# Entry into a state-space loop on Trainium2: three sets of steps reordered, chunk 2's tables built one period sooner

## The chip, the cores and the metric

The kernel runs on one core of a Trainium2 chip. A core has a matrix engine (TensorE, PE in the profile), a vector engine (VectorE, DVE), an activation engine (ScalarE, ACT), a general engine (GpSimd, POOL) and a sync engine that mostly issues DMA transfers (SyncE, SP). Each takes its instructions strictly in the order in which they stand in the program; between engines, semaphores order the work. The metric is the device time of one execution in microseconds (us), the median of the runs shown.

## The reference

A sequence of 2048 positions with 448 channels goes through two branches, mixed by a gate; the kernel returns the mixed output and fourteen gradients.

```python
def fwd(A_u, ..., gate_w):
    x = A_u
    g = sigmoid((x * gate_w).sum(-1, keepdims=True))
    a = S4(x)          # K[d,l] = Re sum_n C dB exp(dt A l); y = causal convolution of u with K, + u * Dskip
    b = MLP(B_x)       # h = relu(x w1 + b1)**2 ; out = h w2 + b2
    return g * a + (1 - g) * b
...
out, vjp = jax.vjp(fwd, A_u, A_A_re, ..., gate_w)
return (out, *vjp(grad_out))
```

The part at issue is the S4 branch's kernel K (448 channels x 2048 positions from 256 complex modes) and, from its gradient dK, the gradients of the modes; and beside it the two layers of the MLP, forward and backward. Positions are rounded to bfloat16, so dK is first summed over positions that round to the same value.

## The kernel before

The middle third of the kernel is a loop over 14 chunks of 32 channels. For each chunk VectorE builds tables of powers: X tables (`step_x`, L656 and L657) and Y tables (`seeds_y`, `build_y`: L723, L670, L673, L679), by doubling from seeds in a record that `load_rec` brings from HBM. ScalarE spreads the record's factors first, `fields_x` (L708, L711) and `fields_y` (L716, L719). Then `kgen` (L752) multiplies X and Y to K, and `k_out` (L759) copies it out.

The backward half of a chunk needs Y transposed (YT). For chunk 0 TensorE turns it (`turn_y`: transposes L788, ScalarE copies L789); for later chunks a DMA transpose does (`load_yt`, L778). `back_z` multiplies YT by a scaled dK (TensorE L814, ScalarE copy L816), `turn_x` turns X (L772), `back_p` multiplies the two on VectorE (L826, L827), `back_s` sums over modes (L843). Scaled dK comes from `scale_a` (ScalarE L795) and `scale_v` (VectorE L799). `psF`, one PSUM tile, is shared by `back_z` and `turn_x`.

**The entry.** Ahead of the loop stand: tables of chunk 0; tables of chunk 1; 116 small matmuls with the weights `Ew` (L1036) that sum the gradient, loaded in four quarters (`load_hs`, L312), to dK; six casts of the sums (L1043); their writes to the scratch tensor `dk_d` (L1047, L1049); two reads of `dk_d` into DK (L1052, L1053), 40 rows and one, on two copies of the partitions; a zeroed row block (L1059, L1060); chunk 0's Y turned; dK scaled; `kgen(0)`.

**The loop.** A string `PERIOD` gives the order of the steps of one period: forward tables of chunk c, backward of chunk c-1, and in between, at each `D`, some steps of the MLP (`dense`). Of the 127 dense steps seven make a block's first layer (`first_layer`: matmuls L904, L907; two ScalarE relus L911; a store L912; two steps later VectorE's square L914) and eight the second (`project`: L880, L882; copy L886; each step half of one output tile). `first_steps = 8` of them fall to period 1; the rest is spread evenly over periods 2 to 13. In period 1 the tables of chunk 1 stand already, so the names in `BUILT` are left out there. The second layer's weights (`w2n`, L1147) are loaded in period 1.

Instructions stand on each engine in the order in which the Python text issues them (`manual_schedule`).

Of the kernel before, what the change touches and what calls it, by code (L numbers as in the profile page):

```python
# [12 lines left out]
ACT = mybir.ActivationFunctionType  # L13
# [6 lines left out]
P = 128  # L20
# [308 lines left out]
def kernel(ctx, tc, A_u, A_A_re, A_A_im, A_B_re, A_B_im, A_C_re, A_C_im, A_log_dt, A_Dskip,  # L329
# [302 lines left out]
    DK = KW[:, NA * D:].rearrange("p (a d) -> p a d", d=D)  # L632
    for h in range(2):
        G_.memset(KW[64 * h + 32:64 * h + 64, NA * D:].bitcast(fp32), 0.0)
    RB = K.t("R32", [P, 16384])
# [215 lines left out]
    w1w = KW[:, 0:7168].rearrange("p (a f) -> p a f", a=DT)  # L851
# [13 lines left out]
    lates = []  # L865

# [28 lines left out]
    def first_layer():  # L895

        rx = [SB[:, 8192:9216], SB[:, 9216:10240], hv[:, 7168:8192], st4]
        for lb in range(4):
            for jp in range(HP):
# [10 lines left out]
                for k in range(2):  # L910
                    S.activation(r[:, 512 * k:512 * k + 512], pss[k][:], ACT.Relu, bias=b1_f[:, 2 * jp + k:2 * jp + k + 1])  # L911
# [84 lines left out]
    for q in range(4):  # L996
        K.load_hs(hd[0], q, hss[q])
    kps = [None]
# [8 lines left out]

    seeds_x(0)
# [5 lines left out]
    load_rec(1)  # L1014
    tables(0)
    fields_x(0)
    fields_x(1)
    tables_y(0)
    nc.sync.dma_start(w1w[:, 0:3], bass.AP(tensor=B_w1.tensor, offset=B_w1.offset, ap=[[F, P], [P * F, 3], [1, F]]))
    for h in range(2):  # L1020
        nc.sync.dma_start(w1w[64 * h:64 * h + 64, 3], bass.AP(tensor=B_w1.tensor, offset=B_w1.offset + 384 * F, ap=[[F, 64], [1, F]]))
# [3 lines left out]
    for i in range(3):  # L1025
        fields_y(i)
    tables_y(1)
# [7 lines left out]
    for k, (x8, g, e, gr) in enumerate(ekeys):  # L1035
        T_.matmul(tiles[e][32 * gr:32 * gr + 32, 0:D], lhsT=ct["Ew"][:, 32 * k:32 * k + 32], rhs=hss[x8 // 2][:, g, x8 % 2, :], start=(k == first[e, gr]), stop=(k == last[e, gr]),  # L1036
                  tile_position=(0, 32 * gr), skip_group_check=True)
    stA, stB = (K.t("st", [P, 4, D], bufs=2) for i in range(2))
    for e in range(6):
# [4 lines left out]
        for l in range(2 if e < 2 else 1):  # L1044
            q = G_ if (e + l) % 2 == 0 else nc.scalar
# [4 lines left out]
    for cpy in range(2):  # L1050
        qe = nc.scalar if cpy else G_
        qe.dma_start(DK[64 * cpy:64 * cpy + 40], bass.AP(tensor=dk_d, offset=0, ap=[[16 * D, 40], [D, 16], [1, D]]))  # L1052
        qe.dma_start(DK[64 * cpy + 40:64 * cpy + 41, 0], bass.AP(tensor=dk_d, offset=640 * D, ap=[[D, 1], [1, D]]))  # L1053

# [4 lines left out]
    G_.memset(zrow, 0.0)  # L1059
    nc.scalar.dma_start(bass.AP(tensor=k_d, offset=16 * 48 * D, ap=[[D, 48], [1, D]]), zrow)  # L1060
# [13 lines left out]
    def spare():  # L1074

        xst[0] += 1
        return K.ps("SX"[xst[0] % 2], [P, 8, P], bf16)
# [561 lines left out]
```

## Time and profile before

| | us |
|---|---|
| median of 3 runs | 816.03 (811.8 to 819.44) |
| profiled execution, its own time | 817.63 |
| its span in the profile | 815.8 |
| TensorE busy in the span | 621.9 (76%) |
| VectorE busy | 625.3 (77%) |
| ScalarE busy | 506.0 (62%) |
| GpSimd busy | 163.9 (20%) |

A row of the timeline gives start, duration, engine, line, operation, what is written and read, the count of instructions merged into it, and in brackets the idle time of the engine just before it with what ended that. `<-DMA` names a transfer that landed. Of a row that merges instructions the duration runs from the first one's start to the last one's end. A row of the windows gives a stretch and its length, then for PE, PEld (weight loads), DVE, ACT and POOL the busy time with a count, then the clock that TensorE was granted (1.00 is full), the share of the DMA engines in use, and GB/s. A row of the groups gives line, engine, operation, tiles and shapes, count, busy us in all, mean ns of one, and idle time before.

### The profile page before, as it was taken

The page shows a single profiled execution, that of the slowest core. Times are in us where ns is not written, and L with a number is a line of the kernel's source. Part 1 is how long each engine was busy: PE and PEld are TensorE (multiplying, and loading weights), DVE is VectorE, ACT ScalarE, POOL GpSimd, SP SyncE. Part 2 cuts the span into 40 slices and gives each one's busy share as a digit, 9 for nine tenths or more (in the row PEclk, how much of TensorE's full clock was granted, in tenths as well). Part 3 has the DMA queues.
Part 4 walks back from the last instruction along what each step waited for, and adds up shares of the span by engine and source line. Part 5 has one row for each costly group of instructions (what it writes and reads, how often), then busy time and mean ns, then how long its engine had stood idle before and what let it go on. Part 6 is the DMA issues. An engine that isn't in the chain of part 4 may idle for free. (4 is left out here: it accounts for less than half of the span.)

```text
span 815.8 us, 16878 instructions
## 1 busy us (share of the span) xinstructions
PE 621.9 (76%) x6749; PEld 299.4 (37%) x6749; DVE 625.3 (77%) x983; ACT 506.0 (62%) x831; POOL 163.9 (20%) x264
## 2 busy tenths in 40 slices
PE   3676467653378889898978978898778788899985
PEld 1222222121234344344534443444534333444442
DVE  3795597877826999999889999998656974687353
ACT  0696567670577676677866766673675577264553
POOL 1222000042111222222321011101034311023112
PEclk9965655575689999899989999999989799799998
DMA  9978866278758577978696979996689998899972
GB/s 193 237 200 279 302 244 231 90 291 208 209 115 180 114 179 167 174 157 191 190 187 119 288 190 251 181 263 162 212 311 324 343 314 282 260 281 330 261 196 64
DMA packets 179694, 178.87 MB, mean 219 GB/s; under 512 B 116549, under 2 KB 157471, under 8 KB 179023
## 3 DMA queue, kind: packets, MB, share of 16 engines
q1 hardware_dynamic: 152632, 101.04, 50.7%
q0 software_dynamic: 17552, 56.44, 22.6%
q10 hardware_dynamic: 9430, 20.31, 7.1%
q8 instruction: 53, 0.87, 0.4%
q14 instruction: 27, 0.21, 0.1%
HBM read 83.67 MB, written 67.53 MB: 185 GB/s over the span
## 5 line engine op out<-in xcount | busy, mean ns | idle before, releaser
L816 ACT CAST P<-psF 128x1024 bf16<-128x1024 f32 x56 | 57.0, 1018 | 36.5 <-PE psF L814 35.9
L656 DVE TENSOR_TENSOR F<-X,F 128x1024 bf16<-128x1024 bf16 (+2 forms) x42 | 64.4, 1533 | 4.1 <-ACT F L711 2.4
L882 PEld LDWEIGHTS <-U 128*128 128x128 bf16 x448 | 40.0, 100 | 52.9 <-issue 15.0
L882 PE MATMUL psN<-D,U 128*128 128x448 bf16 x224 | 52.6, 372 | 6.3 <-DMA D<-in_B_w_dram 3.6
L1196 PEld LDWEIGHTS <-S 128*128 128x128 bf16 x416 | 40.2, 101 | 40.9 <-issue 13.7
L887 POOL DMA_DIRECT2D br_d<-D x32 | 17.9, 560 | 182.7 <-ACT D L886 176.2
L814 PE MATMUL psF<-R,S 41*32 41x256 bf16 x896 | 24.4, 288 | 37.0 <-DVE P L827 16.8
L1196 PE MATMUL psX<-D,S 128*128 128x449 bf16 x224 | 49.4, 365 | 1.5 <-ACT S L1202 1.5
L882 PE MATMUL psN<-S,U 128*128 128x448 bf16 x224 | 48.0, 358 | 2.5 <-DVE U L970 2.4
L826 DVE TENSOR_TENSOR M<-P,psF 128x2048 bf16<-128x2048 bf16 x28 | 34.0, 1215 | 17.1 <-PE psF L772 17.1
L1196 PE MATMUL psX<-K,S 128*128 128x448 bf16 x192 | 43.7, 374 | 1.8 <-ACT S L1199 1.8
L962 PE MATMUL psN<-S,K 128*128 128x512 bf16 x168 | 44.4, 404 | 0.0
L1187 ACT ACTIVATE S<-psN 128x1024 bf16<-128x1024 bf16 x32 | 33.0, 1030 | 14.9 <-PE psN L1183 14.8
L904 PE MATMUL psN<-S,K 128*128 128x512 bf16 x168 | 42.2, 388 | 0.0
L967 ACT ACTIVATE U<-psN 128x512 bf16<-128x512 f32 x56 | 30.8, 605 | 15.5 <-PE psN L965 11.4
L303 PE MATMUL psN<-D,cb_MI 64*128 64x448 bf16 x96 | 31.7, 514 | 9.0 <-DVE D L288 5.7
L886 ACT CAST D<-psN 128x448 bf16<-128x448 f32 x32 | 17.0, 532 | 33.7 <-PE psN L882 33.7
L657 DVE TENSOR_TENSOR X<-F 128x512 bf16<-128x512 bf16 (+2 forms) x42 | 35.6, 849 | 1.4
L772 PE MATMUL psF<-ident,X 128*128 128x128 bf16 x448 | 33.1, 232 | 4.0 <-ACT P L816 3.9
L303 PEld LDWEIGHTS <-cb_MI 64*128 64x128 bf16 x256 | 17.0, 105 | 51.9 <-issue 46.5
L265 PEld LDWEIGHTS <-M 128*64 128x64 bf16 x192 | 13.8, 133 | 60.1 <-issue 53.6
L827 DVE TENSOR_TENSOR P<-P,psF 128x2048 bf16<-128x2048 bf16 x28 | 34.2, 1221 | 1.0
(346 smaller groups left out, 1596.6 us busy)
## 6 DMA issues: line engine op xcount, KB each, us to landing
sp<-K ACTq DMA_DIRECT2D x8, 896.0 KB
dhT_d<-U SPq DMA_DIRECT2D x28, 256.0 KB
R<-sp SPq DMA_DIRECT2D x8, 896.0 KB
S<-dhT_d POOLq DMA_DIRECT2D x14, 512.0 KB, 6.8
R<-hd SPq DMA_DIRECT2D x16, 448.0 KB
S<-rT_d POOLq DMA_DIRECT2D x12, 512.0 KB, 7.0
hd<-st SPq DMA_DIRECT2D x13, 448.0 KB
rec<-rec_d POOLq DMA_DIRECT2D x11, 448.0 KB, 4.6
```

Of the source, the lines that this page charges most:

```text
L303: nc.tensor.matmul(ps[kk2][:, 0:D], lhsT=MI[r0:r0 + 64, m, :], rhs=rh[r0:r0 + 64], start=(k_ == 0), stop=(k_ == len(terms) - 1), tile_posi ...
L656: V.tensor_tensor(out=Vt[:, 0:2 * w * n], in0=run(lo, 0, [0, 2], [NA, w], [1, n]), in1=run(PX[:, 0:1], 512 * k, [2, w], [0, n], [1, 2]), o ...
L657: V.tensor_tensor(out=run(lo, n, [NA * X2, 2], [NA, X2], [1, n]), in0=run(vb, 0, [n * X2, 2], [n, X2], [1, n]), in1=run(vb, (w + X2) * n, ...
L772: T_.transpose(ps[:, t, 128 * b:128 * b + 128], Xs[c % 2][:, o_:o_ + 128], ident[:])
L816: S.copy(zbs[c, g // 2][:, :, g % 2].rearrange("p t h k n -> p t k h n"), psz[:].rearrange("p t (k h n) -> p t k h n", k=2, h=2))
L826: V.tensor_tensor(out=pr.rearrange("p t g h k n -> p t (g h k n)"), in0=zv, in1=xv, op=ALU.mult)
L827: V.tensor_tensor(out=zv, in0=zv, in1=rev_dim(xv, 1), op=ALU.mult)
L882: T_.matmul(ps[:, 0:D], lhsT=hblk[:, j, P * tt:P * tt + P], rhs=ws[:, j, :], start=(w == 1 and j == 0), stop=(j == FT - 1))
L904: T_.matmul(pss[k][:], lhsT=w1w[:, dt, j * P:j * P + P], rhs=UT[:, dt, 512 * lb:512 * lb + 512], start=(dt == 0), stop=False, skip_group_c ...
L962: T_.matmul(pss[k][:], lhsT=w2Tw[:, jp, dt, k], rhs=dblk[:, dt], start=(dt == 0), stop=False, skip_group_check=True)
L1187: S.activation(hn(i)[:, 8 * th:8 * th + 8, :], ps[:], ACT.Square if i < FT else ACT.Copy)
L1196: T_.matmul(ps[:, 0:w], lhsT=hn(i)[:, t, :], rhs=(DB2[:, t, :] if i < FT else U[:, t, 0:w]), start=(t == 0), stop=(t == LT - 1))
```

## The change

1. Chunk 0's Y is turned in parts: groups 0 and 1 after the first and second quarter of the sums, groups 2 and 3 after the writes of dK. Chunk 1's `fields_y` moves in between; its `fields_x` stays ahead of all copies.
2. The load of chunk 1's record and of the first-layer weights is issued ahead of chunk 0's tables, and chunk 2's record behind the reads of DK.
3. dK's rows 640 to 767 of `dk_d` are zeroed at the start by a GpSimd DMA; DK is read in 48 rows a copy, both on SyncE. The writes of dK that were ScalarE's are SyncE's. The zeroed row block is GpSimd's and stands later.
4. Period 1 has an order of its own, `FIRST`: ten dense steps, four of them ahead of `scale_a(0)`; the load of `w2n` behind the first `back_z`; chunk 1's DMA transposes each behind the `back_z` that frees their place; and chunk 2's Y tables, which period 2 then leaves out.
5. In dense steps 5 to 7 the second relu of each is VectorE's (a TENSOR_SCALAR on the PSUM tile).

```diff
+    w1w = KW[:, 0:7168].rearrange("p (a f) -> p a f", a=DT)
     for h in range(2):
         G_.memset(KW[64 * h + 32:64 * h + 64, NA * D:].bitcast(fp32), 0.0)
+    G_.dma_start(bass.AP(tensor=dk_d, offset=640 * D, ap=[[16 * D, 8], [1, 16 * D]]), KW[32:40, NA * D:])
...
                 for k in range(2):
-                    S.activation(r[:, 512 * k:512 * k + 512], pss[k][:], ACT.Relu, bias=b1_f[:, 2 * jp + k:2 * jp + k + 1])
+                    if k and half_dve[0]:
+                        V.tensor_scalar(out=r[:, 512 * k:512 * k + 512], in0=pss[k][:], scalar1=b1_f[:, 2 * jp + k:2 * jp + k + 1], scalar2=0.0, op0=ALU.add, op1=ALU.max)
+                    else:
+                        S.activation(r[:, 512 * k:512 * k + 512], pss[k][:], ACT.Relu, bias=b1_f[:, 2 * jp + k:2 * jp + k + 1])
...
+    rec0 = rec
+    load_rec(1)
+    rec1, rec = rec, rec0
+    nc.sync.dma_start(w1w[:, 0:3], ...)
...
-    load_rec(1)
     tables(0)
+    rec = rec1
     fields_x(0)
     fields_x(1)
     tables_y(0)
-    nc.sync.dma_start(w1w[:, 0:3], ...)
...
     seeds_x(1)
     seeds_y(1)
     tables(1)
-    for i in range(3):
-        fields_y(i)
-    tables_y(1)
...
-    for k, (x8, g, e, gr) in enumerate(ekeys):
-        T_.matmul(tiles[e][...], lhsT=ct["Ew"][...], rhs=hss[x8 // 2][...], ...)
+    for q in range(4):
+        for k, (x8, g, e, gr) in enumerate(ekeys):
+            if x8 // 2 == q:
+                T_.matmul(tiles[e][...], lhsT=ct["Ew"][...], rhs=hss[q][...], ...)
+        if q < 2:
+            YTs[0].append(turn_y(0, q, spare, False))
+        if q == 0:
+            for i in range(3):
+                fields_y(i)
+    tables_y(1)
...
-            q = G_ if (e + l) % 2 == 0 else nc.scalar
+            q = G_ if (e + l) % 2 == 0 else nc.sync
...
     for cpy in range(2):
-        qe = nc.scalar if cpy else G_
-        qe.dma_start(DK[64 * cpy:64 * cpy + 40], bass.AP(tensor=dk_d, offset=0, ap=[[16 * D, 40], [D, 16], [1, D]]))
-        qe.dma_start(DK[64 * cpy + 40:64 * cpy + 41, 0], ...)
+        nc.sync.dma_start(DK[64 * cpy:64 * cpy + SL], bass.AP(tensor=dk_d, offset=0, ap=[[16 * D, SL], [D, 16], [1, D]]))
+    load_rec(2)
-    G_.memset(zrow, 0.0)
-    nc.scalar.dma_start(bass.AP(tensor=k_d, offset=16 * 48 * D, ap=[[D, 48], [1, D]]), zrow)
...
-    YTs[0] = [turn_y(0, g, spare, False) for g in range(NG)]
-    load_rec(2)
-    scale_a(0)
-    scale_v(0)
+    G_.memset(zrow, 0.0)
+    G_.dma_start(bass.AP(tensor=k_d, offset=16 * 48 * D, ap=[[D, 48], [1, D]]), zrow)
+    for g in range(2, NG):
+        YTs[0].append(turn_y(0, g, spare, False))
     kps[0] = kgen(0)
     k_out(0, kps[0])
     PERIOD = """XS X0 YS D Z0 Y0 X1 D X2 Z1 D Y1 T0 SA D P0 LR Y2 D Z2 D Y3 Z3 FX0 Y4 FX1 D S0 FY0 T1 D FY1 FY2 KM P1 SV D D KO S1""".split()
+    FIRST = """D D D D SA SV Z0 L0 W2 FX0 FX1 D Z1 L1 FY0 FY1 FY2 D T0 P0 KM YS Y0 Y1 Z2 L2 D S0 Z3 L3 KO Y2 D T1 P1 D SA2 SV2 Y3 Y4 D S1""".split()
...
-    first_steps = 8
+    first_steps = FIRST.count("D")
+    YBUILT = ("YS", "Y0", "Y1", "Y2", "Y3", "Y4")
     for c in range(1, NCH):
-        for o in PERIOD:
+        for o in FIRST if c == 1 else PERIOD:
             if o == "D":
                 k += 1
+                half_dve[0] = c == 1 and k > 4
...
+            elif c == 1 and o in YBUILT:
+                token(o, 2)
...
-            elif c > 1 or o not in BUILT:
+            elif c != 2 or o not in YBUILT:
                 token(o, c)
```

The first place is ScalarE's stream at the entry. Before, all fields of chunk 1 (they read the record, `M`), then the casts of the sums, with DMA issues between them:

```order
L708 COPY F_181_1339<-M_182_1340 128x2x3x128
L711 ACTIVATE F_181_1339<-M_182_1340 128x3x128 x2
L716 COPY F_181_1339<-M_182_1340 128x6x256
L719 ACTIVATE F_181_1339<-M_182_1340 128x6x64x2 x2
L1043 CAST st_1532<-psN_184_1411 128x448
L1047 DMA dk_d<-st_1532 16x4x448
L1043 CAST st_1532<-psN_185_1412 128x448
L1047 DMA dk_d<-st_1532 16x4x448
```

After, on the same engine from the same instruction on (`R` is the place of YT, `psX` and `psS` hold the turned Y):

```order
L710 COPY F_181_1340<-M_182_1341 128x2x3x128
L713 ACTIVATE F_181_1340<-M_182_1341 128x3x128 x2
L791 COPY R_178_1329<-psX_1422 128x1024
L791 COPY R_178_1329<-psS_1432 128x1024
L718 COPY F_181_1340<-M_182_1341 128x6x256
L721 ACTIVATE F_181_1340<-M_182_1341 128x6x64x2 x2
L791 COPY R_178_1329<-psX_1469 128x1024
L791 COPY R_178_1329<-psS_1479 128x1024
L1063 CAST st_1573<-psN_184_1397 128x448
L1063 CAST st_1573<-psN_185_1398 128x448
```

Four of the eight copies of the turned Y have moved ahead of the casts, but behind the two fields that read chunk 1's record.

The second place is SyncE's stream from the quarters of the gradient (`hd`) on. Before:

```order
L312 DMA P_176_1324<-hd 64x3584 x4
L700 DMA M_182_1340<-rec_d 128x1792
L1019 DMA K_177_1325<-in_B_w_dram 128x3x1792
L1021 DMA K_177_1325<-in_B_w_dram 64x1792 x2
L700 DMA rec_1639<-rec_d 128x1792
L778 DMA_TRANSPOSE R_178_1328<-R_178_1328 128x16x128 x4
```

After:

```order
L312 DMA P_176_1324<-hd 64x3584 x4
L702 DMA M_182_1341<-rec_d 128x1792
L1006 DMA K_177_1325<-in_B_w_dram 128x3x1792
L1008 DMA K_177_1325<-in_B_w_dram 64x1792 x2
L1067 DMA dk_d<-st_1573 16x4x448 x2
L1069 DMA dk_d<-st_1573 16x8x448
L1069 DMA dk_d<-st_1574 1x448
L1071 DMA K_177_1325<-dk_d 48x7168 x2
L702 DMA rec_1591<-rec_d 128x1792
L780 DMA_TRANSPOSE R_178_1329<-R_178_1329 128x16x128 x4
```

Chunk 1's record (`M`) keeps its place behind the quarters; dK's writes and reads have come in, and chunk 2's record (`rec`) stands behind them.

The third place is VectorE's stream in period 1, from the first product of the backward half on. Before (`U` holds the MLP's hidden block, `Y` chunk 2's Y tables):

```order
L826 TENSOR_TENSOR M_182_1340<-P_191_1552,psF_1838 128x2048
L827 TENSOR_TENSOR P_191_1552<-P_191_1552,psF_1838 128x2048
L914 TENSOR_TENSOR U_194_1557<-S_8_163 128x1024
L914 TENSOR_TENSOR U_194_1557<-U_194_1557 128x1024
L914 TENSOR_TENSOR U_194_1557<-st_1556 128x1024
L826 TENSOR_TENSOR M_182_1340<-P_191_1552,psF_1957 128x2048
L827 TENSOR_TENSOR P_191_1552<-P_191_1552,psF_1957 128x2048
L799 TENSOR_TENSOR S_8_163<-S_8_163,vw 128x32x16
```

After:

```order
L828 TENSOR_TENSOR M_182_1341<-P_196_1593,psF_1902 128x2048
L829 TENSOR_TENSOR P_196_1593<-P_196_1593,psF_1902 128x2048
L725 COPY Y_179_1330<-rec_1591 128x2x128
L672 TENSOR_TENSOR F_181_1340<-Y_179_1330,F_181_1340 128x512
L681 TENSOR_TENSOR Y_179_1330<-F_181_1340 128x128x2
L672 TENSOR_TENSOR F_181_1340<-Y_179_1330,F_181_1340 128x1024
L681 TENSOR_TENSOR Y_179_1330<-F_181_1340 128x128x4
L914 TENSOR_SCALAR U_199_1596<-psN_224_2075,b_f 128x512
L919 TENSOR_TENSOR U_199_1596<-S_8_163 128x1024
L672 TENSOR_TENSOR F_181_1340<-Y_179_1330,F_181_1340 128x256x8 x2
L681 TENSOR_TENSOR Y_179_1330<-F_181_1340 128x128x16
L919 TENSOR_TENSOR U_199_1596<-S_8_163 128x1024
```

Chunk 2's Y tables have come between the two pairs of products of period 1; in period 2 the same rows are gone.

38 lines of the change are left out of this document (20 added, 18 removed).

## The prediction

> **What bounds the kernel now.** I read the windows first, a stretch for each period of the loop, then the timeline of each engine around the entry. The chain of waits reaches back only to 740 us and says nothing on this place.
>
> ```profile
> 226.00:255.90 29.90, 21.28 (x438) 10.39 (x436) 9.96 (x13) 23.95 (x37) 6.14 (x8) 0.94 0.74 157
> 255.90:279.00 23.10, 20.68 (x317) 9.76 (x315) 22.59 (x27) 12.48 (x18) 2.74 (x5) 0.85 0.42 90
> 279.00:305.80 26.80, 23.97 (x341) 10.67 (x339) 26.35 (x34) 20.95 (x32) 7.79 (x12) 1.00 0.87 185
> ```
>
> From 255.9 on VectorE is busy 22.59 of 23.10 us and 26.35 of 26.80: the loop runs at its pace. In period 1 (first row) it is busy 9.96 of 29.90. So work counts where VectorE is full, and the entry counts by the moment from which VectorE is full.
>
> ```profile
> 255.99 0.44 DVE L687 COPY X<-rec 128x128 bf16<-128x128 bf16 x1
> ...
> 266.63 1.21 DVE L826 TENSOR_TENSOR M<-P,psF 128x2048 bf16<-128x2048 bf16 x1
> ...
> 276.33 1.21 DVE L826 TENSOR_TENSOR M<-P,psF 128x2048 bf16<-128x2048 bf16 x1
> ...
> 237.82 1.22 DVE L826 TENSOR_TENSOR M<-P,psF 128x2048 bf16<-128x2048 bf16 x1 [2.21 <-PE psF L772]
> ```
>
> These are my marks: chunk 2's tables begin at 255.99, the two products of period 2 at 266.63 and 276.33, the first product of period 1 at 237.82. Behind 276.33 both kernels give VectorE the same work (seven dense squares are done by then in both), so I compare the kernels at that product.
>
> What sets the entry is ScalarE, on whose stream everything passes:
>
> ```profile
> 206.22 0.83 ACT L708 COPY F<-M 128x768 bf16<-128x768 bf16 x1 [21.34 <-DMA M<-rec_d]
> 206.95 0.93 ACT L711 ACTIVATE F<-M 128x384 bf16<-128x384 bf16 x2
> ...
> 214.57 0.94 ACT L1043 CAST st<-psF 128x448 bf16<-128x448 f32 x2 [0.65 <-ACT st L1043]
> ...
> 220.18 1.01 ACT L789 COPY R<-psX 128x1024 bf16<-128x1024 bf16 x1 [4.66 <-POOL P L1059]
> 221.08 1.02 ACT L789 COPY R<-psS 128x1024 bf16<-128x1024 bf16 x1
> ...
> 228.03 2.44 ACT L795 COPY S<-K 128x128 bf16<-128x128 bf16 x4
> ...
> 221.24 1.01 PE L788 MATMUL psX<-ident,Y 128*128 128x128 bf16 x8 [12.68 <-ACT R L789]
> ...
> 230.99 0.41 PE L814 MATMUL psF<-R,S 41*32 41x256 bf16 x16 [2.49 <-DVE S L799]
> ...
> 255.40 1.92 PE L882 MATMUL psN<-D,U 128*128 128x448 bf16 x7 [3.64 <-DMA D<-in_B_w_dram]
> ```
>
> It is idle 21.34 us for chunk 1's record; after the casts it waits 4.66 us for GpSimd's zeroed rows and only then copies the turned Y, eight copies at 0.9 us. TensorE idles 12.68 us for that, and the first `back_z` (call it Z0) starts at 230.99. TensorE also loses 3.64 us to the late second-layer weights.
>
> **Part by part, up to Z0.** Chunk 1's record comes behind the quarters on SyncE as before, so it lands at 206.2 again, and the two `fields_x` still stand ahead of the copies. So turning Y among the sums gains nothing before 206.2. ScalarE: fields until 207.9, two copies (2 x 0.9) until 209.7, `fields_y`, two more copies. TensorE meanwhile cannot go on: the second turn needs `psX` and `psS` emptied, and the third and fourth quarters of the sums now stand behind it. It turns into `psX` after 208.8 and into `psS` after 209.7, at the cold 1.01 us of the row at 221.24, until 210.7. Then 72 sums that before ran at 201:
>
> ```profile
> 201.06 0.55 PE L1036 MATMUL psN<-P,U 128*32 128x448 bf16 x1 [1.64 <-DMA P<-hd]
> ...
> 203.27 1.33 PE L1036 MATMUL psF<-P,U 128*32 128x448 bf16 x6
> ...
> 205.11 0.55 PE L1036 MATMUL psN<-P,U 128*32 128x448 bf16 x4 [0.52 <-DMA P<-hd]
> ...
> 207.01 0.54 PE L1036 MATMUL psF<-P,U 128*32 128x448 bf16 x3
> ...
> 223.50:225.50 2.00, 1.82 (x17) 0.50 0.62 119
> 225.50:227.30 1.80, 1.22 (x18) 0.98 0.23 60
> ```
>
> One half took 201.06 to 204.60 (3.5 us), the other 205.11 to 207.55 (2.4), the first at half clock. I take 5.9 us: the sums end at 216.6 instead of 207.55. The last two rows are windows of TensorE alone while it did nothing but transposes: the granted clock goes from 0.50 to 0.98. [...]
>
> The casts (0.47 us each by the row at 214.57, with no DMA issues between) are held by the sums: end 219.0, before 215.5.
>
> ```profile
> 218.27 0.53 POOL L1052 DMA_DIRECT2D K<-dk_d  x1 [2.33 <-DMA dk_d<-st]
> ...
> DMA to landing us min/median/max: 9.3/9.3/9.3
> ...
> 227.29 1.20 PE L752 MATMUL psX<-Y,X 128*32 128x41 bf16 x128 [0.31 <-ACT R L789]
> ...
> 231.33 1.72 PE L904 MATMUL psN<-S,K 128*128 128x512 bf16 x6
> ...
> 237.55 1.46 PE L904 MATMUL psN<-S,K 128*128 128x512 bf16 x6
> ...
> 239.27 1.47 PE L904 MATMUL psN<-S,K 128*128 128x512 bf16 x6
> ...
> 233.63 1.26 ACT L911 ACTIVATE S<-psN,b_f 128x512 bf16<-128x512 f32 x2 [1.15 <-PE psN L907]
> ```
>
> The last of dK was written at 218.27, 2.8 us after its cast; so now 219.0 + 2.8 = 221.8. The reads of DK took 9.3 us as two transfers of 560 KB side by side on two queues. Now two of 672 KB follow each other on SyncE's. No row has this. From below: the quarters, 896 KB each on the same queue, came 4.05 us apart (201.06 and 205.11), so 1344 KB take 6.1 us, and 2.4 us fixed, estimated by what the row at 218.27 waited: 8.5. From above: twice 9.3 = 18.6. I take 8.5, since the queue and size are those of the quarters: DK at 230.3. Chunk 2's record, half a quarter, follows some 2 us later (232.3), just ahead of its use.
>
> Beside that wait stand four dense steps. After the casts come four copies (3.6 us, to 222.6); `kgen(0)` needs `psX`, emptied at 221.7, and takes 1.2; then four first-layer steps at 1.72 us (from 237.55 to 239.27), to 229.8, and the last relus (1.26) to 231.1. Cold, the six matmuls of a step take 1.72 instead of 1.46; two cold steps would add 0.5 us. ScalarE comes to `scale_a(0)` at 231.1, so DK at 230.3 is just covered; any later, it is paid in full. With 2.44 for `scale_a` and 0.5 for `scale_v` (228.03 + 2.44 = 230.47 to Z0 at 230.99) Z0 starts at 234.1: **3.1 us later than before, with four dense steps done where there were none.**
>
> **From Z0 to the products of period 2.**
>
> ```profile
> 242.25 1.01 ACT L816 CAST P<-psF 128x1024 bf16<-128x1024 f32 x1
> ...
> 245.38 0.28 PE L843 MATMUL psS<-M,cb_sel 128*32 128x256 bf16 x1
> ...
> 245.93 1.07 PE L772 MATMUL psF<-ident,X 128*128 128x128 bf16 x16
> ...
> 272.84 1.74 PE L882 MATMUL psN<-D,U 128*128 128x448 bf16 x7
> ...
> L656 DVE TENSOR_TENSOR F<-X,F 128x1024 bf16<-128x1024 bf16 (+2 forms) x3 | 4.6, 1534 | 0.1
> L670 DVE TENSOR_TENSOR F<-Y,F 128x2048 bf16<-128x2048 bf16 (+2 forms) x4 | 3.6, 930 | 0.1
> L679 DVE TENSOR_TENSOR Y<-F 128x2048 bf16<-128x2048 bf16 (+2 forms) x4 | 3.3, 813 | 0.1
> L657 DVE TENSOR_TENSOR X<-F 128x512 bf16<-128x512 bf16 (+2 forms) x3 | 2.6, 852 | 0.1
> L673 DVE TENSOR_TENSOR F<-Y,F 128x1024 bf16<-128x1024 bf16 x4 | 2.5, 686 | 0.0
> L723 DVE COPY Y<-rec 128x256 bf16<-128x256 bf16 x1 | 0.7, 743 | 0.0
> L914 DVE TENSOR_TENSOR U<-U 128x1024 bf16<-128x1024 bf16 x1 | 0.7, 682 | 0.0
> ```
>
> The first product needs the turned X, which needs `psF`, emptied of the second `back_z`. ScalarE in between: Z0 0.4, copy 1.0, `fields_x` 1.7 (206.22 to 207.9), half a step's relus 0.6, copy 1.0, and on TensorE the turn 1.1: 5.8 us, so 239.9 (before: 237.8). VectorE's half relus are not in the trace; by ScalarE's half (0.63) I take 0.65, between 0.4 and the 1.21 of an L826 that reads twice as many columns from PSUM. Two of the three run before 239.9 beside idle time, one after.
>
> From 239.9 VectorE has, in order: product pair 2.4 (237.82 and its twin); Y tables but their last part, together with it L670, L679, L673, L723 = 10.1; one half relu 0.65; three squares 2.0; product pair 2.4; `scale_v` 0.4, and a wait for it of 0.9, because ScalarE reaches `scale_a(1)` only after a second-layer step's copy that waits for the squares; chunk 2's X tables, 4.6 + 2.6, with 0.6 for their two seed copies as between 255.99 and the next L656. Sum 26.7: the first product of period 2 starts at 266.6, **where it started before (266.63)**. What was saved is spent: the 10.1 us have left period 2, but period 1 was not empty enough for them after Z0, since a wall of VectorE work now begins at 239.9.
>
> The second product, though, had 7.3 us of Y tables in front of it (269.0 to 276.33). Now only TensorE's chain stands there: product pair to 269.0, `back_z` 0.4, half a second-layer step 1.7, `back_z` 0.4, a first-layer step 1.7, `back_s` 0.55 (245.38 to 245.93), turn 1.1: 274.9 instead of 276.33. **Gain 1.4 us.**
>
> Other edits: the weights `w2n` are now asked for right behind the fourth step's store, some 232 instead of 241.6, and are used at some 247; the 3.64 us of waiting go, but TensorE has slack there. Two dense steps fewer in periods 2 to 13 take 3.4 us from TensorE, which is not the bound in the 26.80 us row (23.97). Writes of dK on SyncE stand behind nothing that is late. Zeroing on GpSimd fits into its idle time. I cost these at nothing; if the cover fails, the 3.4 us are gain.
>
> Sum: the profiled 817.6 becomes 816.2; on the median, 816.0 - 1.4, I predict **814.5**.
>
> **Rivals.**
>
> *Z0 is early (faster).* If chunk 1's record lands some 6 us sooner, the turns lie among the sums as written, the sums end at 207.6 as before and Z0 comes at 234.1 - 9 = 225. The marks follow VectorE one for one: 9 + 1.4, some 805.5. For it: the record's transfer is only 448 KB. Against: the order of SyncE is unchanged around it, and it landed 1 us after the last quarter. The same result comes in part if the later periods use the freed TensorE time (3.4 us). 0.18.
>
> *The read of DK is late (slower).* Two reads on one queue, each as slow as 9.3, land at 221.8 + 18.6 = 240.4. It decides from 231.1 on, and from 232.5 it has eaten the gain. Then Z0 is at 243.4, and the time 814.5 + 9.3 = 823.8. For it: 9.3 us for 1120 KB is slow, and nobody hides it. Against: the quarters' pace. [...] Half of such a delay gives 819. 0.18, most of it beyond 820.
>
> *It doesn't do what it says.* The turns wait for the record, so the first part of the change is void; that is already in my forecast. If in addition the four steps run cold throughout (2.1 us each), Z0 is 1.5 us later and the gain is zero: 816. 0.14.
>
> The forecast, 812 to 817, has 0.50.
>
> **How the numbers follow.** A measurement of this kernel tells a change from none at about 1%, 8.2 us: below 807.9 and above 824.2. Faster: most of the first rival, 0.17. Slower: the part of the second with both reads slow and something added, 0.15. Within 1%: 0.68. The range takes in half of either rival and runs from 806 to 823.
>
> **What would show it.** Right: chunk 1's record still ends ScalarE's idle time at some 206; the third quarter's sums start after 210; the read of DK lands near 230 and ScalarE passes from relus to `scale_a` without a wait; Z0 near 234; VectorE without gaps from 240; the second product of period 2 near 275. Wrong: copies of turned Y before 206, a wait of ScalarE for DK, or gaps of VectorE in period 2 as large as the tables that left it.

## The result, and the profile after

The changed kernel takes 829.65 us (median of 16 runs, 819.63 to 840.89), the kernel before beside it 817.2 (16 runs, 809.96 to 821.65): ratio 1.0146, 95% interval 1.0113 to 1.018. The ratio leaves out executions of either kernel that fell into a second, slower state, so it is not the quotient of the two medians. The change is slower, and outside the forecast's range. The profiled execution took 829.21, its span is 827.4.

The windows of the changed kernel, the three stretches that were read of before (columns as there):

```profile
226.00:255.90 29.90, 20.28 (x298) 8.59 (x298) 16.57 (x22) 16.85 (x24) 6.13 (x8) 0.86 1.02 223
255.90:279.00 23.10, 16.79 (x147) 6.83 (x147) 15.36 (x18) 11.53 (x18) 2.76 (x5) 0.81 0.53 109
279.00:305.80 26.80, 24.10 (x336) 10.73 (x336) 24.31 (x31) 20.55 (x33) 8.11 (x12) 0.94 0.40 121
```

VectorE does 6.6 us more in the first stretch and 7.2 less in the second, where it was full (22.59 of 23.10) and is now idle for a third of the time. The work was moved; its end did not come sooner. The timeline of VectorE in the changed kernel, the products of periods 1 and 2 and the end of period 6 (each period has two products):

```profile
243.41 1.21 DVE L828 TENSOR_TENSOR M<-P,psF 128x2048 bf16<-128x2048 bf16 x1
254.75 1.22 DVE L828 TENSOR_TENSOR M<-P,psF 128x2048 bf16<-128x2048 bf16 x1
...
258.82 0.43 DVE L801 TENSOR_TENSOR S<-S,vw 128x512 bf16<-128x512 bf16 x1 [1.60 <-ACT S L797]
...
270.70 1.21 DVE L828 TENSOR_TENSOR M<-P,psF 128x2048 bf16<-128x2048 bf16 x1
...
281.11 1.22 DVE L828 TENSOR_TENSOR M<-P,psF 128x2048 bf16<-128x2048 bf16 x1 [7.94 <-PE psF L774]
...
376.97 2.35 DVE L672 TENSOR_TENSOR F<-Y,F 128x2048 bf16<-128x2048 bf16 x2
379.36 1.22 DVE L681 TENSOR_TENSOR Y<-F 128x2048 bf16<-128x2048 bf16 x1
380.50 0.68 DVE L919 TENSOR_TENSOR U<-U 128x1024 bf16<-128x1024 bf16 x1
...
390.07 1.22 DVE L828 TENSOR_TENSOR M<-P,psF 128x2048 bf16<-128x2048 bf16 x1 [4.62 <-PE psF L774]
```

At the second product of period 2 the loss is 281.11 - 276.33 = 4.8 us. From there to the end of the span it was 815.8 - 276.33 = 539.5 before and is 827.4 - 281.11 = 546.3 now: 6.8 us more. The wait of 4.62 us in period 6 is a part of that. In the timeline of the kernel before, the same product has no wait:

```profile
381.76 1.21 DVE L826 TENSOR_TENSOR M<-P,psF 128x2048 bf16<-128x2048 bf16 x1
```

From the mark to the first product of period 7 it was 121.4 us before and is 124.2 now; the other 4.0 us of the 6.8 lie behind that. A profile shows one execution, and those of one kernel differ by more than that (809.96 to 821.65 us before), so a stretch is trusted here only where it repeats in several profiles.

ScalarE and SyncE's queue at the entry, in the timeline of the changed kernel:

```profile
205.14 0.83 ACT L710 COPY F<-M 128x768 bf16<-128x768 bf16 x1 [21.28 <-DMA M<-rec_d]
...
215.34 1.84 ACT L1063 CAST st<-psN 128x448 bf16<-128x448 f32 x4 [2.05 <-PE psN L1050]
...
220.63 0.78 SPq L1071 DMA_DIRECT2D K<-dk_d  x2
...
229.85 1.26 ACT L916 ACTIVATE st<-psN,b_f 128x512 bf16<-128x512 f32 x2 [0.51 <-ACT U L916]
232.59 2.41 ACT L797 COPY S<-K 128x128 bf16<-128x128 bf16 x4 [1.48 <-issue]
```

The record ends ScalarE's idle time as before, the casts wait for the late sums, and `scale_a` waits 1.48 us behind the last relu for DK, which came 12.0 us after its read was issued (220.63 to the start of `scale_a` at 232.59). TensorE in the changed kernel, behind Z0, in period 2, in period 6 and in period 8:

```profile
235.52 0.63 PE L816 MATMUL psF<-R,S 41*32 41x256 bf16 x16 [5.75 <-DVE S L801]
236.08 2.74 PE L906 MATMUL psN<-S,K 128*128 128x512 bf16 x6
...
273.23 0.63 PE L816 MATMUL psF<-R,S 41*32 41x256 bf16 x16 [6.08 <-DVE P L829]
273.79 2.80 PE L884 MATMUL psN<-D,U 128*128 128x448 bf16 x7
...
377.11 0.51 PE L816 MATMUL psF<-R,S 41*32 41x256 bf16 x16 [2.04 <-DVE P L829]
377.56 1.30 PE L884 MATMUL psN<-D,U 128*128 128x448 bf16 x3
381.24 1.67 PE L884 MATMUL psN<-D,U 128*128 128x448 bf16 x4 [2.38 <-DVE U L919]
...
384.97 2.74 PE L884 MATMUL psN<-D,U 128*128 128x448 bf16 x7
...
443.17 0.63 PE L816 MATMUL psF<-R,S 41*32 41x256 bf16 x16 [5.69 <-DMA R<-R]
443.73 2.80 PE L884 MATMUL psN<-S,U 128*128 128x448 bf16 x7
```

Behind the waits of 5.69 to 6.08 us, and behind the two shorter ones of period 6, a dense step's six or seven matmuls take 2.74 to 2.80 us, where they take 1.47 and 1.50 otherwise. The windows of TensorE alone show why:

```profile
273.20:276.50 3.30, 3.27 (x23) 0.50 0.51 58
384.40:387.50 3.10, 3.10 (x16) 0.50 0.48 133
443.10:446.50 3.40, 3.33 (x27) 0.50 0.73 135
```

The granted clock (the number behind the busy time) is 0.50 there.

### The profile page after: what moved, and what is told of

Same layout as the page of the kernel before. It is cut to its first block, busy times and chain, and to the rows that moved or that the text cites. A ratio compares the mean times of both kernels' runs of the same rounds, so it can differ in the third digit from the quotient of the medians.

```text
span 827.4 us, 16891 instructions
## 1 busy us (share of the span) xinstructions
PE 623.4 (75%) x6749; PEld 299.1 (36%) x6749; DVE 627.6 (76%) x986; ACT 503.6 (61%) x828; POOL 162.9 (20%) x264
## 4 chain that ended last, share of the span: by engine, by line
DVE 24%; PE 21%; DMA 13%; ACT 5%; issue 4%; SPq 1%; POOL 0%; ACTq 0%; DVEq 0%; POOLq 0%
PE psX L1213 8%; DVE F L658 4%; DMA R<-R 3%; PE psN L884 3%; DVE F L672 3%; DVE M L828 2%; DVE P L829 2%; DMA R<-hd 2%; DVE F L675 2%; DVE X L659 2%; DVE U L919 1%; DMA K<-gd 1%; DMA F<-k_d 1%; DVE U L975 1%; PE psN L1200 1%
## 5 line engine op out<-in xcount | busy, mean ns | idle before, releaser
L884 PE MATMUL psN<-D,U 128*128 128x448 bf16 x224 | 55.2, 389 | 6.2 <-DVE U L919 6.1
L884 PE MATMUL psN<-S,U 128*128 128x448 bf16 x224 | 50.7, 372 | 5.1 <-DVE U L975 5.0
L1213 PE MATMUL psX<-D,S 128*128 128x449 bf16 x224 | 47.6, 355 | 1.5 <-ACT S L1219 1.5
L1213 PE MATMUL psX<-K,S 128*128 128x448 bf16 x192 | 41.9, 363 | 1.5 <-ACT S L1216 1.5
L797 ACT COPY S<-K 128x128 bf16<-128x128 bf16 x56 | 34.7, 1007 | 1.5 <-issue 1.5
```

The costliest lines, as they stand in the source:

```text
L797: S.copy(D2[:, :, 0, 4 * l:4 * l + 4].rearrange("p (g i) a -> p a g i", g=NG), DK[:, l::4].rearrange("p a (e g q i) -> p a e q g i", g=NG, ...
L884: T_.matmul(ps[:, 0:D], lhsT=hblk[:, j, P * tt:P * tt + P], rhs=ws[:, j, :], start=(w == 1 and j == 0), stop=(j == FT - 1))
L1213: T_.matmul(ps[:, 0:w], lhsT=hn(i)[:, t, :], rhs=(DB2[:, t, :] if i < FT else U[:, t, 0:w]), start=(t == 0), stop=(t == LT - 1))
```

## The experiments

Three parts of the change came under suspicion: the ten dense steps of period 1, the record that gates the turned Y, and chunk 2's Y tables in period 1. The marks named below are the first instructions of a pair of products, as in the prediction. What some of the expectations call periods 5, 7 and 8 are periods 6, 8 and 9, counted by two products a period.

### Ten dense steps

**Eight steps, all else as changed.**

```diff
-    FIRST = """... Y2 D T1 P1 D SA2 SV2 Y3 Y4 D S1"""
+    FIRST = """... Y2 D T1 P1 SA2 SV2 Y3 Y4 S1"""
```

> The changed kernel with the two last dense steps taken out of FIRST, so that periods 2 to 13 get exactly the dense steps that they had before (8 in period 1). Theory CALENDAR (two dense steps more in period 1 shift the MLP against the chunks, and that costs the waits in periods 5 and 7, some 8 us): those two waits of VectorE (4.6 and 5.1 us) go, the time is 4 us above before, ratio about 1.005. Theory ENTRY (what is lost is lost by the late DK and a cold TensorE in periods 1 and 2, and the later waits follow from any shift in time): the later waits stay, ratio 1.012 to 1.016.

Measured: 1.0049 (1.0017 to 1.008). Behind the second product of period 2 (279.10) 539.5 us follow, as before the change; that they agree to a tenth is chance, since a kernel with ten steps (below, with the Y tables in period 2) has 539.5 too. VectorE and TensorE around period 6, and VectorE at the end of period 1, in the timeline of this kernel:

```profile
376.13 1.22 DVE L681 TENSOR_TENSOR Y<-F 128x2048 bf16<-128x2048 bf16 x1
377.27 0.68 DVE L919 TENSOR_TENSOR U<-S 128x1024 bf16<-128x1024 bf16 x1
...
382.74 1.21 DVE L828 TENSOR_TENSOR M<-P,psF 128x2048 bf16<-128x2048 bf16 x1
...
378.46 1.50 PE L884 MATMUL psN<-D,U 128*128 128x448 bf16 x7
...
257.61 0.42 DVE L801 TENSOR_TENSOR S<-S,vw 128x512 bf16<-128x512 bf16 x1
```

In period 6 there is no wait. Squares stand behind the tables here too, but TensorE, two steps further back, comes to them only at 378.46. With ten steps it is at that projection's second half some steps of the chunk earlier (377.56), waits 2.38 us in the middle of it for squares that start at 380.50 (both above), runs the next half at half clock (2.74 us at 0.50, above), and the turn behind is late. The other wait did not go: in period 8 VectorE still waits 5.72 us here, for the first product instead of the second.

Other profiles say which stretches are the steps'. The wait of period 6 (4.6 to 4.7 us) is in all six changed kernels with ten steps (the change itself and the five variants below that keep ten steps and the places of the later ones), and in none of the five with eight. From the mark to the first product of period 7 those with ten take 124.2 to 124.3 us, four of those with eight 119.6 to 120.0; the fifth, the last kernel of this document, takes 126.4 with a wait of 5.93 us for a DMA transpose. And period 1 is longer with ten: from its first product to that of period 2 27.3 us against 25.6 here, mostly the 1.60 us that VectorE waits for `scale_v` with ten (258.82 above) and not with eight (257.61). So ten steps cost 1.7 us in period 1 and some 4.4 from the mark to period 7.

**Ten steps in the kernel before.**

```diff
-    first_steps = 8
+    first_steps = 10
```

> The kernel before with first_steps = 10 and nothing else: its own entry, the dense calendar of the changed kernel. CALENDAR: some 8 us above before, ratio 1.010, with a wait of VectorE for the turned X in period 5 and one in period 7. ENTRY: ratio 0.998 to 1.002, perhaps a gain from the idle time of period 1.

Measured: 1.0137 (1.0098 to 1.0177). But TensorE's timeline of this kernel has a wait that the changed kernel lacks:

```profile
252.48 2.77 PE L882 MATMUL psN<-D,U 128*128 128x448 bf16 x7 [6.62 <-DMA D<-in_B_w_dram]
```

The first projection now falls into period 1 and waits for `w2n`. So this run alone mixes two causes. VectorE waits 6.43 us in period 3 and 4.97 in period 6; no wait of period 8 came.

**The same with squares held back by one step, not two.**

```diff
-LAG = 2
+LAG = 1
```

> The kernel before with ten dense steps in period 1 (1.0137 alone) and with squares held back by one dense step instead of two. If the calendar costs because the project's second half waits for squares that stand behind Y tables in VectorE's queue (2.70 us in period 5, then a step at 2.80 us and a turn that is 4.97 us late), the wait of the project's half on U in period 5 falls under 1 us, the turn's wait of VectorE under 2 us, and the time falls by 3 to 5 us, to 1.008 to 1.010; the wait in period 3 (a turned Y, 3.77 us) stays. If the place of the project's halves among the chunk's steps does it by TensorE's time alone, or the DMA transposes being late does, the time stays at 1.012 to 1.016.

Measured: 1.0154 (1.0097 to 1.0211). In TensorE's timeline of this kernel the wait for the weights is 16.62 us, and the one for the squares in period 6 is there still:

```profile
262.75 2.77 PE L882 MATMUL psN<-D,U 128*128 128x448 bf16 x7 [16.62 <-DMA D<-in_B_w_dram]
...
390.65 0.93 PE L882 MATMUL psN<-D,U 128*128 128x448 bf16 x2 [2.67 <-DVE U L914]
```

So it is not the holding back that puts squares behind tables. The place of the dense steps remains as the reason; the time of this run, with the weights 10 us later, can't price it.

**The same (with `LAG = 2`) and `w2n` asked for earlier.**

```diff
-            elif c == 1 and o == "LR":
-                G_.dma_start(w2n, ...)
+            elif c == 1 and o == "LR":
+                pass
...
+                if c == 1 and o == "Z0":
+                    G_.dma_start(w2n, ...)
```

> The kernel before with ten dense steps in period 1 and the load of the second layer's weights issued on GpSimd's queue behind the first back step of period 1 instead of behind its first product. In the run with ten steps alone the first projection waited 6.62 us for that load, in another with ten steps 16.6 us, and the changed kernel has no such wait. If ten steps in the kernel before cost 1.0137 mainly by this wait, it goes here and the time is 0.998 to 1.006, and that run did not show what ten steps cost in the changed kernel. If the places of the later steps cost it, the waits of VectorE on psF in periods 3 (6.43 us) and 5 (4.97 us) stay and the time is 1.008 to 1.014.

Measured: 1.0082 (1.0052 to 1.0112); no wait for the weights and none in period 3, but 5.67 us of VectorE in period 6. This is the lower end of the second expectation, with an interval that reaches into the first: ten steps cost the old kernel some 0.8% without the weights, and the weights some 0.5% more (the two intervals overlap).

**Ten steps in period 1, the later steps where eight would put them.**

```diff
-                D_(k if c == 1 else first_steps + (total - first_steps) * (...) // (...))
+                D_(k if c == 1 else 8 + (total - 8) * (...) // (...))
```

> The changed kernel with ten dense steps in period 1, but from period 2 on each dense step at the same place among the chunk's steps as in the kernel before (two places of period 2 stay empty). If ten steps cost because every later step of the perceptron then meets another step of the chunk (projections beside other turns, squares behind other tables), the waits of 4.62 us in period 5 and 5.06 us in period 7 go, the first product of period 8 comes 7 to 9 us sooner than 462.9 and the time is 1.003 to 1.008, as with eight steps. If it costs because period 1 itself is too full, the marks stay 1.5 to 3 us behind the kernel with eight steps alone from period 2 on and no more than that: 1.007 to 1.009. If neither, 1.013 to 1.016.

Measured: 1.0092 (1.0064 to 1.012), between the changed kernel and the one with eight steps. So the places of the later steps are some half of the cost, though this interval just overlaps both others. The shares fit the stretches above: 4.4 us up to period 7 are 0.54% of the time, which is what went, and the 1.7 us of period 1 are a part of what stayed.

### The record that gates the turn

**Chunk 1's fields, seeds and X tables written behind the second early turn.**

```diff
-    rec = rec1
-    fields_x(0)
-    fields_x(1)
     tables_y(0)
-    seeds_x(1)
-    seeds_y(1)
-    tables(1)
...
-        if q == 0:
+        if q == 1:
+            rec = rec1
+            fields_x(0)
+            fields_x(1)
+            seeds_x(1)
+            seeds_y(1)
+            tables(1)
             for i in range(3):
                 fields_y(i)
-    tables_y(1)
+            tables_y(1)
```

> The changed kernel with chunk 1's fields and X tables issued behind the second turn, so that the copies of turned Y stand ahead of the wait for chunk 1's record on ScalarE. ENTRY: copies at 199 to 205, the 72 later sums end at 207 instead of 215.6, DK is read from 215 instead of 220.6, Z0 comes at 230 instead of 235.5, and the time falls by 5 us: ratio 1.008. If Z0 moves but the end does not, the entry is not what the time hangs on.

Measured: 1.0048 (1.0009 to 1.0087), better than the 1.008 expected. ScalarE in this kernel's timeline:

```profile
199.61 1.01 ACT L791 COPY R<-psX 128x1024 bf16<-128x1024 bf16 x1 [15.46 <-PE psX L790]
...
205.62 0.85 ACT L710 COPY F<-M 128x768 bf16<-128x768 bf16 x1
...
227.13 2.41 ACT L797 COPY S<-K 128x128 bf16<-128x128 bf16 x4 [1.54 <-issue]
```

The copies now fill the time in which ScalarE idled; `scale_a` is 5.5 us sooner, and `back_z` with it. In period 2 VectorE still waits 7.82 us for the turn.

**DK read on two queues, GpSimd's and SyncE's.**

```diff
-        nc.sync.dma_start(DK[64 * cpy:64 * cpy + SL], ...)
+        (nc.sync if cpy else G_).dma_start(DK[64 * cpy:64 * cpy + SL], ...)
```

> The changed kernel with the first copy of DK read on GpSimd's queue and the second on SyncE's, side by side as before. If one queue is what made the read take 11.9 us, DK lands 2.5 us sooner, scale_a starts right after the fourth step's relus (1.5 us sooner), and the time falls by 1.5 to 3 us: ratio 1.011 to 1.013. If not the queue: scale_a still waits, ratio as the changed kernel, 1.0146.

Measured: 1.0121 (1.0075 to 1.0168), not told apart from the changed kernel. The timeline of this kernel:

```profile
221.19 0.53 POOL L1071 DMA_DIRECT2D K<-dk_d  x1 [2.82 <-DMA dk_d<-st]
...
234.81 1.86 ACT L797 COPY S<-K 128x128 bf16<-128x128 bf16 x3 [3.97 <-issue]
```

DK is there 13.6 us behind its issue, later than from one queue (12.0), and `scale_a` waits longer (3.97 us instead of 1.48): two reads on one queue are not what makes it slow. The ratio lies in the range of the first expectation, the rows go with the second.

**DK read in 40 rows and one, as before, on SyncE.**

```diff
-        nc.sync.dma_start(DK[64 * cpy:64 * cpy + SL], bass.AP(tensor=dk_d, offset=0, ap=[[16 * D, SL], [D, 16], [1, D]]))
+        nc.sync.dma_start(DK[64 * cpy:64 * cpy + 40], bass.AP(tensor=dk_d, offset=0, ap=[[16 * D, 40], [D, 16], [1, D]]))
+        nc.sync.dma_start(DK[64 * cpy + 40:64 * cpy + 41, 0], ...)
```

> The changed kernel with DK read as before, in 40 rows and one row of one element row, both copies on SyncE. If the read's time goes by its bytes (11.9 us for twice 672 KB in the changed kernel, 9.3 for twice 560 KB in the kernel before), it lands near 230.5 instead of 232.6, scale_a starts right behind the last relu at 231.1 and Z0 is 1.5 us earlier (234.0 instead of 235.5); the end gains 0 to 1.5 us, 1.012 to 1.015. [...]

Measured: 1.0106 (1.0053 to 1.0159), again not told apart from the changed kernel. The timeline:

```profile
219.99 0.29 SPq L1071 DMA_DIRECT2D K<-dk_d  x1
...
230.53 2.41 ACT L797 COPY S<-K 128x128 bf16<-128x128 bf16 x4 [0.55 <-DMA K<-dk_d]
```

`scale_a` starts 10.5 us behind the issue instead of 12.0: 1120 KB instead of 1344, at 107 and 112 KB/us. In the profiles of five changed kernels `scale_a` starts 11.8 to 12.5 us behind the issue of 48 rows on SyncE's queue, so this one read of 40 rows agrees with a time that goes by the bytes, and no more than that.

### The Y tables of chunk 2

**Left in period 2; with eight steps, then with ten.**

```diff
-    FIRST = """... T0 P0 KM YS Y0 Y1 Z2 L2 D S0 Z3 L3 KO Y2 D T1 P1 D SA2 SV2 Y3 Y4 D S1"""
+    FIRST = """... T0 P0 KM Z2 L2 D S0 Z3 L3 KO D T1 P1 D SA2 SV2 D S1"""
-    YBUILT = ("YS", "Y0", "Y1", "Y2", "Y3", "Y4")
+    YBUILT = ()
```

(with eight steps the last two `D` are left out too)

> The changed kernel with eight dense steps in period 1 (1.005 alone) and with the six Y steps of chunk 2 left in period 2, as before. If taking the Y tables out of period 2 is what makes TensorE wait there for the first product (6.08 us), run cold (2.80 us for a step of the project that takes some 1.5 otherwise) and deliver the second turn late (VectorE waits 7.2 to 7.9 us), then with the tables back the wait on psF in period 2 falls under 3 us, the first product of period 2 comes about 3 us later than with eight steps alone (272.5 instead of 269.4), the second at 281 to 282 instead of 279.1, and the time is 1.006 to 1.010: the move is worth 1 to 3 us. If the wait only hands back what the move gains, the second product of period 2 is at 279 to 280 and the time is 1.003 to 1.006.

> The changed kernel with one part undone: the six Y steps of chunk 2 stay in period 2 (ten dense steps in period 1, as changed). With eight steps the same edit brought the second product of period 2 from 279.1 to 273.9, since period 1 got 4.5 us shorter and in period 2 the tables went into the time in which VectorE had waited 7.19 us for the second turn. If the move of the tables is a loss by itself, the wait of 7.94 us on psF in period 2 goes here too, the second product of period 2 comes at 275 to 277.5 instead of 281.1, and the time falls by 3 to 5 us, to 1.008 to 1.011. If it is a loss only together with eight steps (ten steps leave TensorE no idle time in period 2), the second product stays within 2 us of 281.1 and the time at 1.012 to 1.016.

Measured: 1.0006 (0.9968 to 1.0043) with eight steps, 1.006 (1.003 to 1.009) with ten. Better than expected, both times. With eight steps the products of period 2 stand at 264.17 and 273.88, ahead of both expectations; with ten the wait on `psF` goes as expected, but the second product comes at 278.92, later than expected. Periods 1 and 2 of the kernel with ten steps, VectorE and TensorE in its timeline:

```profile
244.81 1.21 DVE L828 TENSOR_TENSOR M<-P,psF 128x2048 bf16<-128x2048 bf16 x1
...
268.28 1.21 DVE L828 TENSOR_TENSOR M<-P,psF 128x2048 bf16<-128x2048 bf16 x1
...
270.66 2.35 DVE L672 TENSOR_TENSOR F<-Y,F 128x2048 bf16<-128x2048 bf16 x2
...
274.31 2.50 DVE L675 TENSOR_TENSOR F<-Y,F 128x1024 bf16<-128x1024 bf16 x4
...
278.92 1.22 DVE L828 TENSOR_TENSOR M<-P,psF 128x2048 bf16<-128x2048 bf16 x1 [0.85 <-PE psF L774]
...
270.80 0.63 PE L816 MATMUL psF<-R,S 41*32 41x256 bf16 x16 [5.23 <-DVE P L829]
```

From product to product period 2 takes 10.6 us with the tables in it and 10.4 without (270.70 to 281.11): TensorE's chain sets it, and the tables fill VectorE's wait. In period 1, from its first product to the first of period 2, it takes 23.5 us without the tables (from 244.81) and 27.3 with them. With eight steps the same pair of kernels gives 9.7 and 9.7 us for period 2, 21.7 and 25.6 for period 1. So in these two pairs the move costs 3.8 to 3.9 us and saves 0.2 at most.

### All of it together

> The changed kernel with both single repairs at once: chunk 1's fields on ScalarE (and its seeds and X tables) written behind the second early turn, and eight dense steps in period 1 in place of ten. If the two losses are separate (the entry's 5 us at Z0, the calendar's 8 us from period 5 on), they add up: 1.0146 - 0.0098 - 0.0097 = 0.995, so 809 to 813 us, the first products of period 2 some 3.5 us before those of the kernel with eight steps alone (269.4 and 279.1), and no wait of VectorE on psF in period 5. If they are one loss seen twice (a chunk that is earlier than the perceptron is the same as a perceptron that is later than the chunk), the second repair brings nothing or spoils the first: 1.002 to 1.008, with a new wait on psF of over 3 us in some period behind period 2.

> Three repairs of the changed kernel together: chunk 1's fields behind the early turn, eight dense steps, and chunk 2's Y tables in period 2; what is left of the change is the two turns among the sums, the 48 rows off ScalarE, the second weights and the second relu halves on VectorE in period 1. If the entry's gain and the tables' are separate, the second product of period 2 comes 5 us before that of the kernel with eight steps and the tables in period 2 (268 to 270 instead of 273.9; 276.3 in the kernel before) and the time is 0.992 to 0.998. If what the entry gains is given back later, as two of the single repairs gave back part of it, the marks of period 8 are level with the kernel before and the time is 0.998 to 1.003.

> The version that is faster than both (chunk 1's fields behind the early turn, eight dense steps, chunk 2's Y tables in period 2: 0.9929) with one part put back: ten dense steps in period 1. If ten steps cost by themselves, whatever else stands in period 1 (1.0146 against 1.0049 in the changed kernel, 0.0097), the time is 0.999 to 1.004, with a wait of VectorE on psF of over 4 us in period 5. If they cost only where period 1 is late and full already (Y tables, late DK), the time is 0.992 to 0.996.

The three join the edits above. The first gave 1.0015, between its two expectations, with the products of period 2 at 264.22 and 272.30, 5.2 and 6.8 us before those with eight steps alone instead of the 3.5 expected. The times of the other two came as expected; the second product of period 2 in the kernel with all three came at 272.19, some 2 us later than expected. With them each combination has a ratio to the kernel before:

| dense steps in period 1 | Y tables of chunk 2 in period | fields ahead of the copies | fields behind the early turns |
|---|---|---|---|
| 10 | 1 | 1.0146 (the change; 1.0113 to 1.018) | 1.0048 (1.0009 to 1.0087) |
| 8 | 1 | 1.0049 (1.0017 to 1.008) | 1.0015 (0.9977 to 1.0053) |
| 10 | 2 | 1.0060 (1.003 to 1.009) | 1.0019 (0.9985 to 1.0052) |
| 8 | 2 | 1.0006 (0.9968 to 1.0043) | **0.9929 (0.9904 to 0.9954)** |

Each repair helps in all four of its pairs, in some by less than the intervals. Averaged over them, the steps are worth 0.7 of a hundredth, the tables 0.6, the fields 0.6; from all to none it is 2.2. They are not one loss seen three times. A second repair brought only 0.3 to 0.5, the third again 0.8 or 0.9, but that isn't shown to be more than scatter: if the three averages are simply added around the mean of the eight, each of the eight ratios comes out within 0.2 of a hundredth, inside its interval. The last kernel beats both: 808.87 us beside 815.53. What else is left of the change in it (the early turns, the 48 rows, the weights, the relus on VectorE) was not priced one by one. And in one pair the cost of the tables is not seen at the mark: with the fields moved and eight steps, the second product of period 2 stands at 272.30 with the tables in period 1 and at 272.19 with them in period 2; there only the times speak for it. VectorE in the kernel with all repairs but the eight steps, period 6:

```profile
381.06 1.22 DVE L828 TENSOR_TENSOR M<-P,psF 128x2048 bf16<-128x2048 bf16 x1 [4.56 <-PE psF L774]
```

And in the kernel with all three, the two products of period 2:

```profile
259.71 1.22 DVE L828 TENSOR_TENSOR M<-P,psF 128x2048 bf16<-128x2048 bf16 x1
...
272.19 1.22 DVE L828 TENSOR_TENSOR M<-P,psF 128x2048 bf16<-128x2048 bf16 x1 [2.69 <-PE psF L774]
```

With ten steps the wait of period 6 is there, although period 1 is no longer late and holds no tables: the steps cost by themselves. With eight, period 2's products stand 6.9 and 4.1 us ahead of the kernel before.

**The best kernel with the 40-row read.**

> The version that is faster than both (0.9929) with the read of DK in 40 rows and one, on SyncE, in place of 48. In that version scale_a waited 2.50 us for the read and began at 228.0; in the changed kernel the same edit let the read land 10.5 instead of 12.0 us behind its issue and scale_a begin 2.1 us sooner, of which 0.6 came ahead of the issue. If the read goes by its bytes, scale_a begins at 226.5 here and the time is 0.990 to 0.993, the most to be had being 1.5 us. If Z0's time is not what holds period 1 in this version (TensorE's chain or VectorE's work is), the read is shorter and the time stays at 0.9929 within 0.002.

Measured: 0.9927 (0.9898 to 0.9956). `scale_a` begins at 227.47, right behind the last relus, instead of at 228.00 behind a wait of 2.50 us, and the time stays. Half a microsecond at the entry can't be told here.

## Why the prediction was wrong

**What held.** The record did land at 205.1 and the fields ahead of the copies made the early turn void. Second turn (209.7 against 210.7), sums, casts (218.0 against 219.0) and the writes (220.6 against 221.8) each came as computed, 1 us early with the whole run; the third and fourth quarters' sums took 6.0 us, 5.9 were taken. That this cost 9 us of sums was in the sum; the run with the fields moved confirms the path: 5.5 us at `scale_a`, 0.6 of a hundredth on average.

**The step that failed: "behind 276.33 both kernels give VectorE the same work".** And with it "I cost these at nothing; if the cover fails, the 3.4 us are gain", said of the two dense steps. VectorE's work is the same, but the dense steps meet other chunk steps from period 2 on. I counted their TensorE time and not their order. Of the 11.6 us of span, 6.8 lie behind the mark: 2.8 up to the first product of period 7, where ten steps cost 4.1 to 4.7 us against eight in all four pairs, and 4.0 behind that, where single profiles differ too much to assign them. On average 544.5 us follow the mark in the six changed kernels with ten steps (539.5 to 548.7), 537.8 in the five with eight (532.9 to 543.2). The times say the same: ten steps cost 0.7 of a hundredth on average, and they cost it in a kernel where nothing else is late, too. A sign was wrong here: I had allowed only for a gain.

**Mis-sized, all to one side, up to the mark.** Predicted 274.9, measured 281.1:
- DK: 8.5 us taken from the quarters' pace, 12.0 measured; the row of the same read before, 9.3 for 1120 KB, scaled by bytes gives 11.2 and was the nearer one. `scale_a` was not "just covered" but waited 1.48. Z0 came at 235.52 instead of 234.1.
- Z0 to the first product: 5.8 against 243.41 - 235.52 = 7.9. TensorE had idled 5.75 us, and the dense step behind Z0 took 2.74 us at a clock of 0.50. The row of 1.72 us at 231.33 that I took for a cold step had run at a clock of 1.00 until past 232 and at 0.50 only from 232.5.
- VectorE's wall: 26.7 against 27.3, with the wait for `scale_v` at the place foreseen (1.60 measured behind the second pair, 0.9 taken). This was right, and it says already that the tables cost period 1 their full length.
- TensorE's chain in period 2: 5.9 against 7.94 of waiting. The chain was the right successor, but its steps were taken too short. The projection step behind the first product took 2.72 us up to the next `back_z` instead of 1.7, the first-layer step 2.3 instead of 1.7, at a clock of 0.50 to begin with, after 6.08 us of idling. The kernel before shows it in small, in TensorE's timeline of period 2:

```profile
269.15 0.41 PE L814 MATMUL psF<-R,S 41*32 41x256 bf16 x16 [2.42 <-DVE P L827]
269.49 2.38 PE L882 MATMUL psN<-D,U 128*128 128x448 bf16 x7
```

So the gain of 1.4 us became a loss, and undoing the move showed it: 3.8 us of period 1 for nothing.

**The rivals.** *Z0 early* did not occur as the change was written; with the fields moved it does, by 5.5 us and not by 9. *The read of DK late* was right in kind (12.0 us, not 18.6) and small in effect: shortening it in the best kernel changed nothing. *It doesn't do what it says* was right for the early turn. Its Z0, 1.5 us later than forecast, is also what came (1.4), but by luck: of the four steps only the first was cold (2.29 us, at a clock of 0.50 from 222.0 to 223.5, then 1.47 three times at 1.00), ScalarE came to `scale_a` at 231.1 as forecast, and it was DK that delayed Z0.

No run shows 48 rows to be read faster than 40: 10.5 us for 40 rows and 12.0 for 48 are much the same KB/us (107 and 112).

**Open.** What of the time behind period 7 is the steps' and what the DMA transposes'. TensorE's longest wait for a transpose between 240 and 612 us is 5.69 us in the changed kernel (in period 8), 7.3 and 3.1 in two of the variants with ten steps, 4.9 and 2.8 in two of those with eight; in the best kernel with the 40-row read one of 7.12 us stands in period 8. No run changed the transposes alone.

## What to carry to other kernels

When work is moved out of a full stretch, look up what the other engine's chain takes there, at the clock that it will have after waiting (here 0.50 behind waits of 5.69 to 6.08 us): if the chain is as long as the stretch, the work was free where it stood and costs where it goes. Filler that runs beside a pipeline has a place as well as an amount; shifting it by two steps moves every later step onto another neighbour, so compare its order against the main steps periods later, and not its sum. When a step is written earlier, read which instruction stands ahead of it on its engine's queue, since one wait for data ahead of it makes the move void (here ScalarE's 21.28 us for chunk 1's record).

## What the runs showed of the hardware

- Behind waits of 5.69 to 6.08 us TensorE's clock in the changed kernel is 0.50 for over 4 us (235.5 to 240.5, 273.2 to 278.0, 443.1 to 448.5): 2.74 to 2.80 us for a step that takes 1.47 or 1.50 otherwise. It was seen behind shorter waits, too: in period 6 of the changed kernel the clock is 0.50 from 377.5 on, behind one wait of 2.04 us, and stays so through the next wait until 387.5; in period 2 of the kernel before it is 0.50 from 270.0 to 273.0, behind a wait of 2.42 us.
- Two reads of DK on SyncE's queue are there, by the start of `scale_a`, 10.5 us (1120 KB, one profile) and 11.8 to 12.5 us (1344 KB, five profiles) behind their issue; with one of the two on GpSimd's queue, 13.6 us (1344 KB, one profile).
- The load of the second layer's weights, issued at the same place of the program, kept TensorE waiting 6.62 us in one kernel and 16.62 us in another that differ only in when VectorE squares: the load itself took 12.2 us in the first, and the projection that waited began at 252.48 and at 262.75, one profile each.
